# Sigmoid attention and two MoE layers: a conditional wait before the last scatter, sums of squares on VectorE, and two steps moved

## The chip, the core and the metric

The kernel runs on one core of one Trainium2 chip, as one program. Its time is the device time of one execution in microseconds (us), and less is better. The profile is of one execution; its times count from the first instruction. TensorE does the matmuls, VectorE and ScalarE the elementwise work, GpSimd some of it and the indirect DMA, and SP (SyncE) issues most DMAs.

## The reference

Four batches of 448 tokens pass through sigmoid attention (12 heads of 64), then through a first layer of experts that only tokens with a positive skip score enter, then through a second one for all tokens. Each token goes to one of eight experts and is scaled by that expert's gate. The second layer routes by normalized rows, which is where the sums of squares come from.

```
x = attention(q, k, v)                       # 1792 x 768
# layer 1: tokens with x @ w_skip > 0
e = argmax(xc @ w_gate);  y = gate_w * (relu(xc @ w1[e]) @ w2[e]);  out = x + y
# layer 2: all tokens
xn = x / (norm(x) + 1e-6);  en = emb / (norm(emb) + 1e-6)
e = argmax(xn @ en.T / tau);  out = gate_w * (relu(x @ v1[e]) @ v2[e])
```

With the reference's inputs nearly all tokens of a batch choose the same expert. In layer 1 no token of batches 0 and 1 is computed, all 448 of batch 2 go to expert 4, and of batch 3 407 go to expert 3 and 41 to expert 7. In layer 2 the four batches go to experts 5, 3, 6 and 2, but for 5 tokens of batch 2 that go to expert 1.

## The kernel before

**Dense blocks.** A batch's most frequent expert is computed for the whole batch, in a "dense block". The 1024 hidden columns come in eight groups f of 128. `h(f)` makes a group of the hidden layer (18 matmuls of 448 columns: six chunks, each in three products of high and low parts), ScalarE writes its high part `hh` (L820) and VectorE its low part `hl` (L821) out of a PSUM bank, and `y(f)` adds that group's share to six output banks `YS` (again 18 matmuls). The order in the code is the order on every engine; nothing is rescheduled:

```
h(f);  sub(2f);  y(f - 1);  sub(2f + 1)
```

So "step k" of a block is `sub(k)`: an even step stands between `h(f)` and `y(f - 1)`, an odd one between `y(f - 1)` and `h(f + 1)`. In the steps other work is issued: first the block's own weights (`units1`, `units2`: loads on SP, and L790 and L791, which split them into high and low parts on ScalarE and VectorE), then the lists that `merge` puts together, in the order given. Two PSUM banks (`BANKS`) serve `h` and all small matmuls of the steps. `bank()` hands them out in turn, so a second small matmul in one step gets the bank of the `h` just before it.

**Sums of squares.** For each batch `raw` copies the rows of x (ScalarE, L1098), `squares` squares six tiles of 128x448 (ScalarE, L1104), and `squares_sum` adds them into the tile `G` (GpSimd, five adds, L1108). The routing step `s1` (L250) reads `G` on TensorE. `route2_steps` returns the list of all that: three pieces `halves` (L702, L703), then `raw`, `squares`, `squares_sum`, `s1`, `s2`, `s3` (L293, L294, L296), `scaled_logits`, `gates`. `ROUTED` says at which steps of the second layer's blocks j = 0 and j = 1 the part from `raw` on stands for batches 1, 2 and 3; batch 0's sum stands at the end of the first dense block.

**The gate product.** In the second layer's blocks j = 0, 1, 2, `gate_tokens` builds the gates in the token order that the output needs: `ready` at step 3 (VectorE, L362 to L366, then L1359, which writes `SEL`), and `turned` at step 8 (TensorE L1366, which reads `SEL`, and a copy, L1368). GpSimd scales the block's output by it at the end (L1379). For j = 0, step 3 also holds a pair of `halves` pieces ahead of `ready`.

**Items.** Tokens that did not choose the batch's main expert are computed apart, in "items" of up to 64 or 32 tokens. `item_list` makes their list in three parts; part two ends with two VectorE operations L460, which write `SEL`, and part three reads that in four small matmuls (L468) and writes the list `LI` (L472 to L484). In the first dense block the parts stand at steps 10, 12 and 15; a batch's list entry is loaded by the engines when they decide which code runs next (L1263, behind the decision L1278). SP makes the same loads before it issues the next weights (L494, L499).

**The end.** The last block (j = 3) has a layer-2 item beside it. `finish_last` stores the batch in two halves (L1414), and `put` scales the item's rows (`xg`, L1028) and scatters them with an indirect DMA from GpSimd (L1029). An explicit dependency makes the scatter wait for the first store, and the tracking of `out` makes it wait for the second. Behind it stands the end of the If (L1494) and one more If for further items (L1506), which is empty here.

Of the kernel before, what the change touches and what calls it, by code (L numbers as in the profile page):

```python
# [14 lines left out]
ALU = mybir.AluOpType  # L15
AX = mybir.AxisListType
ENG = mybir.EngineType
# [4 lines left out]
def sigmoid_attention_moe_moe_kernel(  # L22
# [15 lines left out]
    nc = tc.nc  # L38
    B, H, S, D = q.shape
    NE, DM, DF = w1.shape  # L40
    NT = B * S
# [3 lines left out]
    ND = DM // 128  # L45
# [12 lines left out]
    raw = ctx.enter_context(tc.tile_pool(name="raw", bufs=1))  # L58
# [30 lines left out]
    K = {}  # L89
# [425 lines left out]
    def merge(*steps):  # L515

        out = {}
        for t in steps:
            for k in sorted(t):
                f = t[k]  # L520
                out.setdefault(k, []).extend(f if isinstance(f, list) else [f])
        return out
# [169 lines left out]
    R1, R2 = Route(0), Route(1)  # L692
# [169 lines left out]
    def halves():  # L862

        hw = DM // 2
        n = TL[0]
        for t in range(2):
            r, o = slice(n * t, n * t + n), slice(t * hw, t * hw + hw)
            nc.scalar.activation(YW[:n, o], YS[0][r, :hw], AF.Copy, scale=GS[r, 0:1])
        for t in range(2):
            r, o = slice(n * t, n * t + n), slice(t * hw, t * hw + hw)  # L870
            nc.vector.scalar_tensor_tensor(
                YW[n:, o], YS[0][r, :hw], GS[r, 0:1], YW[:n, o].bitcast(F32), op0=ALU.mult, op1=ALU.subtract
            )

    def spread(b):

        for d in range(ND):
            ps = YS[d]
            nc.tensor.matmul(ps[:, :S], lhsT=YW[:, d * 128 : (d + 1) * 128], rhs=SELT, start=True, stop=True)
            xd = batch_cols(d, b)  # L880
            nc.vector.tensor_add(xd, xd, ps[:, :S])
# [7 lines left out]
    class Item:  # L889
# [127 lines left out]
                            start=s + g + i == 0, stop=ng * s + g + i == 4,  # L1017
                        )

        def put(self):  # L1020
            if self.m == 0:
                halves()
                spread(self.b)
                return
            w = DM // self.ng
            nc.vector.scalar_tensor_tensor(IDX, GS[:, 1:2], float(self.ng), K["pc"][:, 7:8], op0=ALU.mult, op1=ALU.add)
            yg = spare()[:, :w]
            nc.vector.tensor_scalar(yg, YS[0][:, :w], GS[:, 0:1], None, op0=ALU.mult)  # L1028
            sc = nc.gpsimd.indirect_dma_start(  # L1029
                out=out.rearrange("n (t d) -> (n t) d", t=self.ng),  # L1030
                out_offset=bass.IndirectOffsetOnAxis(ap=IDX[:, 0:1], axis=0),
                in_=yg, in_offset=None, bounds_check=self.ng * NT - 1, oob_is_err=False,
            )
            return sc

        def ready(self, k0):

# [58 lines left out]
    def raw(b):  # L1096
        for p in range(ND):
            nc.scalar.activation(XR[:, p], batch_cols(p, b), AF.Copy)  # L1098

    SQ = ROW[:, : ND * S].rearrange("p (c s) -> p c s", s=S)  # L1100
# [3 lines left out]
            nc.scalar.activation(SQ[:, p], XR[:, p], AF.Square)  # L1104

    def squares_sum():
        for p in range(1, ND):
            nc.gpsimd.tensor_tensor(K["G"], K["G"] if p > 1 else SQ[:, 0], SQ[:, p], op=ALU.add)  # L1108

    def batch_of(j):  # L1110
        return nc.values_load(K["pb"][0:1, 8 + j : 9 + j], engines=XENG, min_val=0, max_val=B - 1)
# [32 lines left out]
    def next_dense(j):  # L1144

        box = {}
        xs = XST[(j + 1) % 2]

        def start():
            box["b"], box["e"] = rest_regs(j)  # L1150
            load1(w1, box["e"], 0)
            load2(w2, box["e"], 0)
            gate_cols(R1, box["b"])

        def rows():
            gate_rows(bank("ps_G"))
            box["p"] = split_gated(xs, box["b"])
            for p in range(2):
                box["p"](p)

        def last():
            load_unit(w1, w2, box["e"], 1)
            for f in split_unit(0)[:3]:
                f()

        return {
            8: start, 10: rows, 11: lambda: [box["p"](p) for p in (2, 3)], 12: lambda: [box["p"](p) for p in (4, 5, 6)], 13: last,
            14: lambda: [f() for f in split_unit(0)[3:]],
        }
# [115 lines left out]
    def item_steps(R, at):  # L1285
        return at_subs(at, item_list(R))
# [21 lines left out]
    with tc.If(na > 0) as cmp:  # L1308
        b, e = FIRST["b"], FIRST["e"]
        early = {0: s1, 2: s2, 4: s3, 5: [pl[0], lambda: gates(R1, B - 1, B)()], 6: pl[1], 7: pl[2]}  # L1310
        dense(XST[0], beside(units1(e), early), 0, NF // 2)
        NB["n"] = nb_load()
        with tc.If(NB["n"] > 0) as cmp2:
            steps = merge(next_dense(0), item_steps(R1, (10, 12, 15)), {12: lambda: raw(batch_of(0)), 15: squares})
            dense(XST[0], beside(units1(e), steps), NF // 2)
            add_y(b)
            squares_sum()
            block1(1)
        with cmp2.Else():
            steps = merge(rest2(), item_steps(R1, (9, 11, 12)))  # L1320
            dense(XST[0], beside(units1(e), steps), NF // 2)
            add_y(b)
            leftovers_now(lambda: start2(True))
            rare()
# [27 lines left out]
    def gate_tokens(j, box):  # L1352

        a = SEL[:P, :128]

        def ready():
            g = dense_gate(R2, j)
            four = [P, 4, C, 8]
            nc.vector.tensor_tensor(  # L1359
                a.rearrange("p (g c r) -> p g c r", g=4, r=8), g.unsqueeze(1).unsqueeze(3).to_broadcast(four),  # L1360
                K["seg"][:P].unsqueeze(1).unsqueeze(1).to_broadcast(four), op=ALU.mult,
            )

        def turned():
            ps = bank("ps_gt")
            nc.tensor.matmul(ps[:, :NK], lhsT=a, rhs=K["off"][:P], start=True, stop=True)  # L1366
            t = box["gt"] = sm.tile([128, NK], F32, tag="gtt", name="gtt", bufs=1)
            nc.vector.tensor_copy(t, ps[:, :NK])  # L1368

        return {3: ready, 8: turned}  # L1370

    def finish(j, b, gt):

# [18 lines left out]
    def finish_last(j, b):  # L1392
# [54 lines left out]

    pend, STORES = None, []
    ROUTED = {
        0: [(1, (1, 2, 2, 5, 6, 8, 10, 11)), (2, (7, 7, 7, 11, 12, 14, 15, 15))],  # L1450
        1: [(3, (3, 7, 7, 9, 10, 12, 13, 15))],
    }
    assert B == 4
    for j in range(B):
        box = {"e": e}
        last = j == B - 1
        if last:
            todo = {}
        else:
            todo = at_subs((3, 5, 7), route2_steps(j + 1, XST[(j + 1) % 2])[:3])  # L1460
            for n, at in ROUTED.get(j, ()):
                todo = merge(todo, at_subs(at, route2_steps(n, None)[3:]))
            todo = merge(todo, gate_tokens(j, box))
        if j == 0:
            load_unit(v1, v2, e, 1)
            halves()
            for f in split_unit(0, FIRST_RAW)[3:]:
                f()
            todo = merge({-0.5: lambda: spread(item_b())}, todo)
        if j == B - 2:  # L1470
            todo = merge(todo, item_steps(R2, (9, 11, 13)))
        if pend:
            todo = merge({2: pend}, todo)

        def units2(k):
            u, r = k // 4, k % 4
            if r == 0 and u + 2 < NU:
                load_unit(v1, v2, box["e"], u + 2)
            if k == 10 and not last:
                box["n"] = expert_of(j + 1)  # L1480
                load_unit(v1, v2, box["n"], 0)
            if (u + 1 < NU or not last) and r % 2 == 0:
                for f in split_unit((u + 1) % NU)[:3] if r == 0 else split_unit((u + 1) % NU)[3:]:
                    f()
            if k == 12 and not last:
                load_unit(v1, v2, box["n"], 1)

        xs = XST[j % 2]
        if not last:
            dense(xs, beside(units2, todo))  # L1490
            pend = finish(j, b, box["gt"])
            b, e = nc.values_load(K["pb"][0:1, 9 + j : 10 + j], engines=[ENG.SP], min_val=0, max_val=B - 1), box["n"]
            continue
        with tc.If(count(R2) > 0) as cmp:  # L1494
            it = Item(1, 0)
            at, prep = it.ready(0)
            steps = schedule(merge(todo, at), prep, (5, 5, 7))
            dense(xs, beside(units2, steps), end=finish_last(j, b))
            it.finish([None] * 3)
            info = mybir.DependencyInfo(mybir.DependencyClass.Sync, mybir.DependencyReason.DATA)  # L1500
            tc.add_manual_dep(it.put().ins, STORES[0].ins.name, info, reason="the rows it lands on")
        with cmp.Else():
            STORES = []
            dense(xs, beside(units2, todo), end=finish_last(j, b))
# [36 lines left out]
```

## Time and profile before

| | us |
|---|---|
| median of three timed runs | 561.24 (561.08 to 562.42) |
| profiled execution | 561.57 |
| its span, first to last instruction | 559.7 |
| TensorE matmul busy | 541.7 (97%) |
| VectorE busy | 296.8 (53%) |
| ScalarE busy | 251.2 (45%) |
| GpSimd busy | 79.5 (14%) |

The 1.87 us between span and time lie around the profiled instructions. The page names the engines PE (TensorE matmul), PEld (weight load), DVE (VectorE), ACT (ScalarE), POOL (GpSimd) and SP; a "q" behind the name is the engine's sequencer. A busy TensorE is one whose matmuls overlap, so the waits in brackets, and the spacing of starts, tell more than the busy share. The first attention stage lasts until about 150 us, the first layer until about 290, the second until the end.

### The profile page before, as it was taken

What the parts mean: (1) busy time and instruction counts of PE and PEld (TensorE: products, weight loads), DVE (VectorE), ACT (ScalarE), POOL (GpSimd) and SP (SyncE); (2) the same over time, 40 slices, a digit from 0 to 9 for tenths busy, and PEclk for the clock granted to TensorE, in tenths of its full rate; (3) what the DMA queues carried; (4) which work ended last, traced back from release to release, by engine and by line L of the source; (5) the groups of instructions that cost most, each with busy time, mean ns of one, the idle gap of its engine ahead of it and who ended that gap; (6) DMA issues with size and microseconds to landing.
All of it is one profiled execution on the core that took longest, in us unless ns stands there. A gap on an engine that the chain in (4) does not pass through costs nothing. (4 is left out here: it accounts for less than half of the span.)

```text
span 559.7 us, 10157 instructions
## 1 busy us (share of the span) xinstructions
PE 541.7 (97%) x3663; PEld 424.9 (76%) x3663; DVE 296.8 (53%) x794; ACT 251.2 (45%) x407; POOL 79.5 (14%) x153
## 2 busy tenths in 40 slices
PE   8999999999999998999989989999999999999993
PEld 5564644545489887899759878999899998989882
DVE  3734435246858676673138757694486534543221
ACT  5766776766932473231118543175133422222120
POOL 5010000000000013363002240043003000305000
PEclk9999999999999999999999999999999999999998
DMA  9868566764360603334557006227423832464263
GB/s 181 144 123 138 104 117 110 141 107 145 138 202 2 219 10 131 113 102 155 185 170 269 19 5 237 99 50 219 169 73 92 217 112 78 117 147 168 99 227 105
DMA packets 169244, 73.35 MB, mean 131 GB/s; under 512 B 134450, under 2 KB 160838, under 8 KB 169168
## 3 DMA queue, kind: packets, MB, share of 16 engines
q1 hardware_dynamic: 147440, 65.71, 43.7%
q10 hardware_dynamic: 21360, 6.20, 4.6%
q0 software_dynamic: 368, 0.53, 0.5%
q8 instruction: 36, 0.59, 0.4%
q14 instruction: 40, 0.33, 0.2%
HBM read 66.90 MB, written 5.60 MB: 130 GB/s over the span
## 5 line engine op out<-in xcount | busy, mean ns | idle before, releaser
L820 ACT ACTIVATE hh<-bank 128x448 fp32r<-128x448 f32 x48 | 26.1, 543 | 198.6 <-PE bank L802 168.5
L800 PE MATMUL bank<-xs,h 128*128 128x448 f32 x288 | 106.9, 371 | 2.5 <-DVE xT L1197 1.0
L800 PE MATMUL y<-hh,h 128*128 128x448 f32 x288 | 107.2, 372 | 0.0
L802 PE MATMUL bank<-xs,l 128*128 128x448 f32 x288 | 105.5, 366 | 1.0 <-issue 0.9
L802 PE MATMUL y<-hh,l 128*128 128x448 f32 x288 | 105.5, 366 | 0.0
L801 PE MATMUL y<-hl,h 128*128 128x448 f32 x288 | 105.4, 366 | 0.0
L801 PE MATMUL bank<-xs,h 128*128 128x448 f32 x288 | 105.3, 366 | 0.0
L821 DVE SCALAR_TENSOR_TENSOR hl<-bank,hh 128x448 fp32r<-128x448 f32 x48 | 29.9, 622 | 133.4 <-ACT hh L820 133.3
L621 ACT ACTIVATE A<-psS,bias 128x896 f32<-128x896 f32 x84 | 83.3, 1006 | 34.8 <-PE psS L617 34.5
L791 DVE TENSOR_TENSOR l<-r,h 128x512 fp32r<-128x512 f32 (+1 forms) x115 | 91.5, 844 | 3.7 <-ACT h L790 1.9
L617 PE MATMUL psS<-qT,kT 64*64 64x448 f32 x672 | 87.3, 541 | 0.5 <-ACT A L621 0.3
L635 PE MATMUL psO<-A,v 64*64 64x448 f32 x672 | 86.3, 539 | 0.0
L790 ACT ACTIVATE h<-r 128x512 fp32r<-128x512 f32 (+1 forms) x115 | 74.4, 708 | 0.0
L800 PEld LDWEIGHTS bank<-xs,h 128*128 128x128 f32 x288 | 54.1, 188 | 12.7 <-issue 5.2
L635 PEld LDWEIGHTS psO<-A,v 64*64 64x64 f32 x672 | 34.8, 133 | 32.2 <-issue 19.9
L800 PEld LDWEIGHTS y<-hh,h 128*128 128x128 f32 x288 | 54.1, 188 | 5.3 <-issue 0.6
L802 PEld LDWEIGHTS bank<-xs,l 128*128 128x128 f32 x288 | 54.1, 188 | 5.0 <-DVE l L791 0.4
L801 PEld LDWEIGHTS y<-hl,h 128*128 128x128 f32 x288 | 54.1, 188 | 4.7 <-issue 0.2
L802 PEld LDWEIGHTS y<-hh,l 128*128 128x128 f32 x288 | 54.1, 188 | 4.7
L801 PEld LDWEIGHTS bank<-xs,h 128*128 128x128 f32 x288 | 54.1, 188 | 4.3
L617 PEld LDWEIGHTS psS<-qT,kT 64*64 64x64 f32 x672 | 32.4, 132 | 30.6 <-issue 16.2
L1108 POOL TENSOR_TENSOR G<-row 128x448 f32<-128x448 f32 x4 | 5.1, 1264 | 250.3 <-ACT row L1104 233.6
(267 smaller groups left out, 449.8 us busy)
## 6 DMA issues: line engine op xcount, KB each, us to landing
r<-in_moe_w_dram SPq DMA_DIRECT2D x62, 768.0 KB, 4.7
k<-in_k_dram SPq DMA_DIRECT2D x44, 112.0 KB, 2.8
q<-in_q_dram SPq DMA_DIRECT2D x44, 112.0 KB, 3.1
v<-in_v_dram ACTq DMA_DIRECT2D x44, 112.0 KB, 2.8
out_dram<-row SPq DMA_DIRECT2D x12, 336.0 KB, 3.8
stg<-in_moe_w_dram SPq DMA_DIRECT2D x1, 768.0 KB, 6.9
row<-in_moe_w_dram SPq DMA_DIRECT2D x1, 768.0 KB, 7.8
out_dram<-row SPq DMA_DIRECT2D x1, 672.0 KB, 3.9
```

Source lines behind the costliest of these rows:

```text
L617: nc.tensor.matmul(ps[KT * i : KT * i + KT, j, :S], lhsT=kT[r, i, h * KT : (h + 1) * KT], rhs=qT[r, i], start=True, stop=True,)
L621: nc.scalar.activation(at, ps[:, :, :S], AF.Sigmoid, bias=bias, scale=1.0 / math.sqrt(D))
L635: nc.tensor.matmul(ST[w, "o"][i][D * j : D * j + D, :S], lhsT=t[r, j, h, :], rhs=at[r, j, :], start=h == 0, stop=h == NH - 1,)
L790: nc.scalar.activation(dst_h, src, AF.Copy)
L791: nc.vector.tensor_sub(dst_l, src, dst_h.bitcast(F32))
L800: nc.tensor.matmul(ps, lhsT=ah, rhs=bh, start=first, stop=False)
L801: nc.tensor.matmul(ps, lhsT=ah, rhs=bl, start=False, stop=False)
L802: nc.tensor.matmul(ps, lhsT=al, rhs=bh, start=False, stop=last)
L820: nc.scalar.activation(a, ps[:, :S], AF.Relu)
L821: nc.vector.scalar_tensor_tensor(l, ps[:, :S], 0.0, a.bitcast(F32), op0=ALU.max, op1=ALU.subtract)
L1108: nc.gpsimd.tensor_tensor(K["G"], K["G"] if p > 1 else SQ[:, 0], SQ[:, p], op=ALU.add)
```

## The change

Four edits. The item's scatter is taken out of `put` and issued in one of two branches on GpSimd: if the item belongs to the last batch, with the dependency on the stores as before, otherwise without any on them. `squares_sum` runs on VectorE, in three operations: one over half of the tiles at once (128x1344), and two of 128x448. The list's third part in the first dense block moves from step 15 to step 13. In the second layer's block j = 0 the gate product's `turned` moves from step 8 to step 4, and the sum for batch 2 from step 7 to step 9.

```diff
-        def put(self):
+        def put(self, scatter=True):
...
-            sc = nc.gpsimd.indirect_dma_start(
+            self.yg = yg
+            return self.scatter() if scatter else None
+
+        def scatter(self):
+            return nc.gpsimd.indirect_dma_start(
...
     def squares_sum():
-        for p in range(1, ND):
-            nc.gpsimd.tensor_tensor(K["G"], K["G"] if p > 1 else SQ[:, 0], SQ[:, p], op=ALU.add)
+        n = ND // 2
+        nc.vector.tensor_add(SQ[:, :n], SQ[:, :n], SQ[:, n:])
+        for p in range(1, n):
+            nc.vector.tensor_add(K["G"], K["G"] if p > 1 else SQ[:, 0], SQ[:, p])
...
-            steps = merge(next_dense(0), item_steps(R1, (10, 12, 15)), {12: lambda: raw(batch_of(0)), 15: squares})
+            steps = merge(next_dense(0), item_steps(R1, (10, 12, 13)), {12: lambda: raw(batch_of(0)), 15: squares})
...
-        return {3: ready, 8: turned}
+        return {3: ready, 8 if j else 4: turned}
...
-        0: [(1, (1, 2, 2, 5, 6, 8, 10, 11)), (2, (7, 7, 7, 11, 12, 14, 15, 15))],
+        0: [(1, (1, 2, 2, 5, 6, 8, 10, 11)), (2, (7, 7, 9, 11, 12, 14, 15, 15))],
...
             it = Item(1, 0)
+            own = nc.values_load(R2.LI[0:1, 0:1], engines=[ENG.Pool], min_val=0, max_val=B - 1)
...
             it.finish([None] * 3)
+            it.put(False)
             info = mybir.DependencyInfo(mybir.DependencyClass.Sync, mybir.DependencyReason.DATA)
-            tc.add_manual_dep(it.put().ins, STORES[0].ins.name, info, reason="the rows it lands on")
+            with tc.If(own > B - 2) as cmp2:
+                tc.add_manual_dep(it.scatter().ins, STORES[0].ins.name, info, reason="the rows it lands on")
+            with cmp2.Else():
+                sc = it.scatter()
+                for st in STORES:
+                    tc.declare_no_dep(sc.ins, st.ins, reason="rows of another batch")
```

## Rows read from the trace of the kernel before

**Rows 1.** The page, busy us (share of the span) and instructions of TensorE and others.

```profile
PE 541.7 (97%) x3663; PEld 424.9 (76%) x3663; DVE 296.8 (53%) x794; ACT 251.2 (45%) x407; POOL 79.5 (14%) x153
```

**Rows 2.** Timeline of TensorE, block j = 0: start, us, line, tiles, idle before.

```profile
307.82 0.36 PE L800 MATMUL y<-hh,h 128*128 128x448 f32 x1
...
324.77 0.39 PE L294 MATMUL bank<-OH,one 112*128 112x32 f32 x2
326.99 0.39 PE L1366 MATMUL bank<-off,sel 112*128 112x14 f32 x2 [1.83 <-DVE hl L821]
327.24 0.45 PE L800 MATMUL y<-hh,h 128*128 128x448 f32 x1
...
331.55 0.47 PE L800 MATMUL bank<-xs,h 128*128 128x448 f32 x1 [0.43 <-DVE tt L296]
```

**Rows 3.** Timeline of TensorE, the same place in block j = 1.

```profile
406.38 0.39 PE L294 MATMUL bank<-OH,one 112*128 112x32 f32 x2
406.60 0.45 PE L800 MATMUL y<-hh,h 128*128 128x448 f32 x1
```

**Rows 4.** Timeline of TensorE, first dense block and the seam to `block1`.

```profile
201.22 0.36 PE L800 MATMUL bank<-xs,h 128*128 128x448 f32 x1
...
213.87 0.44 PE L800 MATMUL bank<-xs,h 128*128 128x448 f32 x1 [0.96 <-DVE xT L1197]
...
216.03 0.36 PE L802 MATMUL bank<-xs,l 128*128 128x448 f32 x1 [0.91 <-issue]
```

**Rows 5.** Timeline of VectorE, the list of the first layer's items.

```profile
201.85 0.53 DVE L460 TENSOR_SCALAR sel<-io,ilf 128x64 f32<-128x64 f32 x2
...
212.14 1.03 DVE L484 CAST LI<-ilm 1x4 int32<-1x4 f32 x1
```

**Rows 6.** The chain that ended last, its last piece: start, us, what.

```profile
555.62 0.89 POOL out_dram L1029
```

**Rows 7.** Timeline of VectorE and of GpSimd at the end.

```profile
550.72 0.42 DVE L1028 TENSOR_SCALAR xg<-y,small 128x192 f32<-128x192 f32 x1 [1.78 <-PE y L1014]
...
555.40 1.10 POOL L1029 DMA_INDIRECT out_dram<-xg,small  x1 [39.13 <-SPq L1506]
```

**Rows 8.** The scatter's line L1029, from issue to landing.

```profile
DMA to landing us min/median/max: 2.9/2.9/2.9
```

**Rows 9.** Lines L1494 and L1506, TensorE's sequencer: ns min/median/max, first to last start.

```profile
L1494 PEldq COMPARE_BRANCH  x2: 73/2558/5043, 478.4 to 549.4; - x2
...
L1506 PEldq COMPARE_BRANCH  x1: 3119/3119/3119, 555.0 to 555.0; - x1
```

**Rows 10.** Timeline of VectorE, blocks j = 0 and j = 1.

```profile
306.49 2.49 DVE L703 TENSOR_TENSOR xs<-xT,xs 128x448 fp32r<-128x448 f32 x2 [1.74 <-ACT xs L702]
...
311.30 0.29 DVE L1359 TENSOR_TENSOR sel<-dg,seg 112x128 f32<-112x128 f32 x1
...
313.85 0.62 DVE L703 TENSOR_TENSOR xs<-xT,xs 128x448 fp32r<-128x448 f32 x1
...
372.50 1.14 DVE L703 TENSOR_TENSOR xs<-xT,xs 128x448 fp32r<-128x448 f32 x2
...
374.22 0.29 DVE L1359 TENSOR_TENSOR sel<-dg,seg 112x128 f32<-112x128 f32 x1
...
384.33 0.95 DVE L791 TENSOR_TENSOR l<-r,h 128x768 fp32r<-128x768 f32 x1
```

**Rows 11.** Timeline of ScalarE, the squares of batch 1 in block j = 0.

```profile
303.09 2.90 ACT L1104 ACTIVATE row<-stg 128x448 f32<-128x448 f32 x6
```

**Rows 12.** Line L1278, TensorE's sequencer.

```profile
L1278 PEldq COMPARE_BRANCH  x1: 3796/3796/3796, 209.0 to 209.0; - x1
```

**Rows 13.** Timeline of SP, first weight load of `block1`.

```profile
214.27 0.38 SPq L494 DMA_DIRECT2D r<-in_moe_w_dram  x1
```

**Rows 14.** Two stretches: us, busy by engine (instructions), granted clock, DMA share, GB/s.

```profile
209.00:212.80 3.80, 3.80 (x20) 3.30 (x18) 3.48 (x10) 1.00 (x3) 3.56 (x4) 1.00 0.02 6
549.40:554.50 5.10, 1.18 (x32) 0.65 (x20) 0.42 (x1) 0.00 (x0) 0.00 (x0) 1.00 0.47 141
```

More of the change, by code (lines that the diff above doesn't have):

```diff
@@ L1028, in put @@
             nc.vector.tensor_scalar(yg, YS[0][:, :w], GS[:, 0:1], None, op0=ALU.mult)
-            sc = nc.gpsimd.indirect_dma_start(
+            self.yg = yg
+            return self.scatter() if scatter else None
+        def scatter(self):
+            return nc.gpsimd.indirect_dma_start(
                 out=out.rearrange("n (t d) -> (n t) d", t=self.ng),
                 out_offset=bass.IndirectOffsetOnAxis(ap=IDX[:, 0:1], axis=0),
-                in_=yg, in_offset=None, bounds_check=self.ng * NT - 1, oob_is_err=False,
+                in_=self.yg, in_offset=None, bounds_check=self.ng * NT - 1, oob_is_err=False,
             )
-            return sc
         def ready(self, k0):
```

## The prediction

> **What bounds the kernel now.** I read the page first: TensorE is busy for 541.7 of 559.7 us [rows 1], so the time moves only where TensorE waits, or behind its last matmul. I therefore went through TensorE's timeline by the "idle before" in brackets, and then, for each place that the diff touches, through VectorE, ScalarE and GpSimd beside it. Three places count.
>
> First, the second layer's first dense block (j = 0). There the gate product's matmul L1366 at step 8 waits 1.83 us for VectorE's `hl`, since the routing matmuls L293 and L294 just took the other bank; it starts at 326.99 though L294 ran at 324.77. A little later the next `h` waits 0.43 us for L296, which is late on VectorE [rows 2]. In the next block (j = 1) the step after L294 starts 0.22 us behind it [rows 3]: that is the spacing without a wait.
>
> Second, the seam from the first dense block to `block1`: TensorE stops for 0.96 and, five matmuls on, for 0.91 us [rows 4]. The first is put down to VectorE's L1197; the register load of L1263 stands there too, and the list that it reads is only written by L484, which ends at 213.17 [rows 5].
>
> Third, the end. The chain that ended last is the scatter alone [rows 6]: GpSimd idles for 39.13 us and issues it at 555.40, while its data (`xg`) stands at 551.14 [rows 7], and it lands 2.9 us later [rows 8], at 558.3. But TensorE, whose matmuls are over, is not done either: its jump at the end of the If (L1494) takes 5.04 us, to 554.5, and the jump over the last If (L1506) 3.12 us from 555.0, to 558.15 [rows 9].
>
> **The change part by part.**
>
> *The scatter's wait.* In the reference's data the one item of the second layer holds five rows of batch 2, and the last block is batch 3, so the branch without the wait is taken. The scatter can then go from 551.2 on and land by about 554.1 to 555. What is late next is TensorE's second jump, 558.15 against 558.3: I take -0.1. The new branch stands on GpSimd, behind the gathers and some 35 us ahead of the data, so its load and jump are covered by that same 39 us. The bounds are 0 and, if the two jumps also became shorter, 558.3 - 555 = -3.3. The Trainium skill (NRT & Kernel Launch, "Instruction fetch mechanics") states that a taken branch with its target outside the fetched window waits for a DMA of the target page; the two jumps of 5.04 and 3.12 us agree, and the rule speaks against any gain here.
>
> *The sums of squares.* Four times, five GpSimd adds become three VectorE adds. A 128x768 operation of this kind takes 0.95 us and a 128x448 one 0.62 [rows 10], so 1.03 ns per column: the first add (1344 columns) costs 1.56, the other two 0.62 each, 2.8 us together. VectorE has room, and a late `hl` is covered: y(f) reads it only after a block of y and a block of h, each about 3.9 us (y from 327.24, the next h due at 331.1 [rows 2]). So three of the sums (batch 0 at the seam, batch 2 at step 9, batch 3 at step 7) I cost at nothing; without that cover each costs up to 2.8. The one for batch 1 at step 2 stands in front of something, next. In exchange the operations beside GpSimd's adds get quicker: the pair of L703 took 2.49 us there and 1.14 elsewhere [rows 10]. The Trainium skill (SBUF — State Buffer, "Who interferes with whom") says that a VectorE instruction with two SBUF inputs contends with a GpSimd instruction that reads SBUF, and the pair agrees; by that rule alone one would forecast a gain, which is the second rival below.
>
> *The gate product from step 8 to step 4 for j = 0.* What goes: y(3) starts at 324.99 instead of 327.24, -2.25, and since one bank less is taken there, the next h no longer follows L296: -0.43 [rows 2, 3]. What comes: step 4 stands right behind h(2), which ends as y(1) starts, at 307.82 [rows 2]. The product reads what L1359 writes in step 3, and in the kernel before L1359 ended at 311.59 [rows 10]; that held nothing up, as TensorE wanted it only at step 8. Now VectorE's order is: sum of squares (step 2), a pair of L703, three small operations and L1359. ScalarE's last square ends at 305.99 [rows 11]. Add 2.8 for the sum, 308.8; the pair and the products behind it took 2.01 where GpSimd was idle (372.50 to 374.51 [rows 10]), 310.8. TensorE then takes L1366, and y(1) 0.25 later (326.99 to 327.24 [rows 2]): 311.05 instead of 307.82, **+3.2**. Bounds: if the adds were free, 308.0 for the product, so +0.4; if pair and products ran as slowly as beside GpSimd's adds (306.49 to 311.59, 5.1 us [rows 10]), 313.9 and +6.3. I stay near the quick end, since what ran beside them is gone.
>
> *The list's third part from step 15 to step 13 (first layer).* Its four matmuls L468 now stand between y(5) and h(7), which starts at 201.22 [rows 4]. They read what the two L460 write, and these end at 202.38 on VectorE, which has no slack ahead of them [rows 5]. So h(7) is held about **+1.2**; the matmuls themselves cost the same in either place. Bounds: 0 (the list were ready) and +1.5. What the earlier list gives: L484 moves up by some 5 us, so the register load at the seam finds it. Of the 0.96 us this could return 0.3 (213.17 against the jump's end: L1278 starts at 209.0 and takes 3.80, to 212.8 [rows 12]). I count it at 0, because the stop five matmuls later waits for no data ("issue") and would take up what comes earlier.
>
> *What the earlier list sets off.* SP waits for the same list, and its next weight loads start 1.1 us behind it, at 214.27 [rows 13]. They move to about 209, in front of TensorE's jump, which shifts to about 210.2. Before, the DMA share during that jump was 0.02, and the jump took 3.80; the jump at L1494, with the last store in flight, had a share of 0.47 and took 5.04 [rows 9, 12, 14]. The difference is 1.24. TensorE runs out of matmuls just as this jump ends, so each tenth more is idle time. I take **+1.0**, near the row with traffic; bounds 0 and, with two loads in flight instead of one store, 2.5.
>
> *The step of batch 2's sum (7 to 9)* only keeps VectorE from waiting for the squares in front of `hl`; nothing.
>
> **The sum**: -0.1 + 3.2 - 2.25 - 0.43 + 1.2 + 1.0 = +2.6 us. It is made against the profiled execution (span 559.7, 561.57 with what lies around it); that execution is 0.33 above the median of 561.24, so I put the change on the median: **563.8 us**.
>
> **The rivals.**
>
> *The jump is not delayed* (the loads start later than I think, or leave room): +1.6, 562.8 us. For it: no row shows a jump beside weight loads. Against it: the 5.04 of L1494 beside a store.
>
> *Faster: the two moved pieces are ready when TensorE gets there.* Then only what goes is left: -2.25 - 0.43 - 0.1 + 0.25 for L1366 in its new place = -2.5, 558.7 us. The point that decides is L1359 before 307.8, three microseconds earlier than my chain. For it: free of GpSimd's adds VectorE's pair alone gains 1.3 us. Against it: the last square ends only at 305.99, and behind that the sum, the pair and the products are 4.8 us in one queue. If the end fell by 3.3 as well or instead, this case grows.
>
> *One of the two waits is missing*: without the product's 2.6 - 3.2 + 0.25 = -0.35 (560.9), without the list's +1.4 (562.6).
>
> *The jump waits for both loads*: 2.5 instead of 1.0, 565.3 us and above.
>
> *The change does not do what it says*: were the branch with the wait taken, only the -0.1 would go.
>
> **How the numbers follow.** A measurement of this kernel tells about 0.3% (1.7 us) from no change. My forecast gets 0.46 (all of it slower, 562.95 to 564.7); no delay of the jump 0.22 (0.08 slower, 0.14 within); one wait missing 0.13 (0.12 within, 0.01 slower); neither wait or a shorter end 0.12 (faster); both loads 0.07 (slower). That makes slower 0.62, within 0.26, faster 0.12. The range reaches down to one wait missing and up to the jump behind both loads, 560.8 to 565.6, and leaves out the faster case and a little above.
>
> **What would show it.** L1366 of j = 0 behind h(2) with some 3 us idle and VectorE's L1359 as its releaser; no wait at step 8 and none before h(5). L468 ahead of h(7) with 1.2 us idle put down to L460. SP's load at the seam near 209, ahead of TensorE's jump of L1278, and that jump longer than 4 us. The scatter issued near 552, the span's last microsecond unchanged behind TensorE's L1506. No G adds on GpSimd, and L703 at 0.6 each. I am wrong if L1366 finds its product, if the jump stays at 3.8, or if the two jumps at the end shrink.

## The result, and the profile after

The changed kernel takes 568.74 us (median of 5 runs, 566.19 to 569.53) beside 561.84 (561.08 to 563.09) for the kernel before: a ratio of 1.0111 [1.0082, 1.0140], slower. (Ratios here are of means, with 95% intervals.) The forecast was 563.8 with a range of 560.8 to 565.6, so the side was right and the size was not: 6.9 us more instead of 2.6. The profiled execution took 569.53, its span is 567.7, 8.0 more than before. It is the slowest of the five, so what is read from it adds up to somewhat more than the 6.9 of the medians.

The page of the changed kernel, busy us and share of the span:

```profile
PE 547.2 (96%) x3663; PEld 428.9 (76%) x3663; DVE 298.5 (53%) x806; ACT 251.2 (44%) x407; POOL 54.5 (10%) x133
```

The same 3663 matmuls are busy 5.5 us longer than before [rows 1]. A wait can't do that. Work or clock must have changed, and the matmuls are the same.

TensorE's timeline after, first layer (L1202 was L1197):

```profile
201.92 0.49 PE L468 MATMUL bank<-sel,pc 128*1 128x64 f32 x4 [0.83 <-DVE sel L460]
...
216.02 0.46 PE L800 MATMUL bank<-xs,h 128*128 128x448 f32 x1 [2.44 <-DVE row L1111]
...
216.86 0.57 PE L800 MATMUL bank<-xs,h 128*128 128x448 f32 x1
...
218.72 0.74 PE L800 MATMUL bank<-xs,h 128*128 128x448 f32 x1 [0.54 <-issue]
```

and in the second layer's block j = 0 (L1371 was L1366):

```profile
315.92 0.61 PE L1371 MATMUL bank<-off,sel 112*128 112x14 f32 x2 [2.90 <-DVE sel L1364]
316.36 0.72 PE L800 MATMUL y<-hh,h 128*128 128x448 f32 x1
...
336.09 0.39 PE L294 MATMUL bank<-OH,one 112*128 112x32 f32 x2
336.31 0.45 PE L800 MATMUL y<-hh,h 128*128 128x448 f32 x1
...
340.10 0.36 PE L800 MATMUL bank<-xs,h 128*128 128x448 f32 x1
```

The waits stand where they were forecast: a new one of 0.83 us at L468 for L460, 2.44 instead of 0.96 at the seam, and a new one of 2.90 at the gate product for the operation that writes its operand (L1364, L1359 before). The stop that followed the seam's first one shrinks from 0.91 to 0.54 us. The two old waits, at step 8 and at the next h [rows 2], are gone. But look at the second number of each line: behind 2.44 and behind 2.90 a matmul of 448 columns takes 0.57 and 0.72 instead of 0.36 and 0.45. Windows of the changed kernel say why; the columns are us, busy by engine, granted clock, DMA share, GB/s:

```profile
209.80:215.40 5.60, 3.78 (x19) 3.17 (x17) 4.82 (x7) 1.38 (x3) 0.00 (x0) 1.00 0.81 278
216.55:223.38 6.83, 6.29 (x18) 5.07 (x17) 0.48 (x1) 0.00 (x0) 0.00 (x0) 0.50 0.02 5
315.54:322.36 6.82, 6.44 (x18) 5.79 (x19) 3.78 (x8) 0.54 (x2) 0.00 (x0) 0.50 0.00 0
324.60:331.40 6.80, 6.80 (x36) 6.23 (x35) 2.10 (x3) 3.15 (x6) 0.00 (x0) 1.00 0.00 0
```

From 0.5 us behind the one stop, and from 0.4 us ahead of the end of the other, the granted clock stands at 0.50, which is 1.2 of 2.4 GHz, for 6.8 us each: 18 matmuls instead of the 36 of the last line. In the profiled execution of the kernel before it stands at 1.00 from 5.5 to 555 us without a break.

SP's load and TensorE's jump at the seam (L1283 was L1278), in the changed kernel:

```profile
208.56 0.39 SPq L494 DMA_DIRECT2D r<-in_moe_w_dram  x1
```

```profile
L1283 PEldq COMPARE_BRANCH  x1: 5616/5616/5616, 209.8 to 209.8; - x1
```

The load is issued at 208.56 instead of 214.27 [rows 13], the DMA share during the jump is 0.81 instead of 0.02 [rows 14], and the jump takes 5.62 instead of 3.80 us [rows 12].

VectorE in the second layer, from the sum to the product's operand:

```profile
311.05 1.56 DVE L1111 TENSOR_TENSOR row<-row 128x1344 f32<-128x1344 f32 x1 [1.27 <-ACT row L1107]
312.64 0.62 DVE L1113 TENSOR_TENSOR G<-row 128x448 f32<-128x448 f32 x1
313.30 0.62 DVE L1113 TENSOR_TENSOR G<-G,row 128x448 f32<-128x448 f32 x1
313.85 1.15 DVE L703 TENSOR_TENSOR xs<-xT,xs 128x448 fp32r<-128x448 f32 x2
...
315.57 0.29 DVE L1364 TENSOR_TENSOR sel<-dg,seg 112x128 f32<-112x128 f32 x1
```

This is the forecast queue, with the forecast durations: 2.8 us of sums, and a pair that takes 1.15 instead of 2.49 [rows 10]. The Trainium skill (SBUF — State Buffer, "Who interferes with whom") puts such a pair's slowness down to GpSimd's reads; the trace agrees, the gain is there, and the product still comes 2.9 us late.

The end, GpSimd's scatter and TensorE's two jumps:

```profile
560.47 1.10 POOL L1033 DMA_INDIRECT out_dram<-xg,small  x1 [35.55 <-DVE xg L1028]
```

```profile
L1508 PEldq COMPARE_BRANCH  x1: 5123/5123/5123, 557.9 to 557.9; - x1
...
L1518 PEldq COMPARE_BRANCH  x1: 2744/2744/2744, 563.5 to 563.5; - x1
```

The scatter now waits for `xg` alone and lands 2.7 us later, at 563.2; TensorE's second jump ends at 566.2. The time moved out of the scatter, and TensorE's code is last.

The account in the profile: how far the starts of TensorE's blocks stand behind those of the kernel before, step by step.

| step | forecast, us | measured, us |
|---|---|---|
| list part at step 13 (L468), with the 0.14 by which the first layer starts early | +1.2 | +0.8 |
| jump at the seam (+1.4), and the second stop (0.54 instead of 0.91 us) | +1.0 | +1.1 |
| **clock at half behind the seam** | none | **+2.8** |
| until the second layer | 0 | +0.3 |
| gate product at step 4 | +3.2 | +3.5 |
| **clock at half behind the product** | none | **+2.8** |
| step 8, the next h | -2.7 | -2.8 |
| until TensorE's last block, and the end | -0.1 | -0.5 |
| sum | +2.6 | +8.0 |

Without the two lines in bold the measured sum is 2.4.

### The profile page after: what moved, and what is told of

It reads as the page before. It is cut to its first block, busy times and chain, and to the rows that moved or that the text cites. A ratio compares the mean times of both kernels' runs of the same rounds, so it can differ in the third digit from the quotient of the medians.

```text
span 567.7 us, 10128 instructions
## 1 busy us (share of the span) xinstructions
PE 547.2 (96%) x3663; PEld 428.9 (76%) x3663; DVE 298.5 (53%) x806; ACT 251.2 (44%) x407; POOL 54.5 (10%) x133
## 4 chain that ended last, share of the span: by engine, by line
PE 88%; DVE 4%; ACT 3%; DMA 2%; issue 2%; DVEq 0%; POOL 0%; SPq 0%; POOLq 0%; ACTq 0%
PE y L800 10%; PE psS L617 10%; PE bank L800 10%; PE y L801 10%; PE y L802 10%; PE psO L635 10%; PE bank L802 10%; PE bank L801 10%; PE y L1014 1%; PE bank L989 1%; DMA r<-in_moe_w_dram 1%; PE bank L250 1%; ACT A L621 1%; DMA k<-in_k_dram 1%; PE ps_r L250 1%
## 5 line engine op out<-in xcount | busy, mean ns | idle before, releaser
L800 PE MATMUL bank<-xs,h 128*128 128x448 f32 x288 | 108.2, 376 | 4.4 <-DVE row L1111 2.4
L800 PE MATMUL y<-hh,h 128*128 128x448 f32 x288 | 108.4, 376 | 0.0
L802 PE MATMUL bank<-xs,l 128*128 128x448 f32 x288 | 106.7, 370 | 0.1
L801 PE MATMUL bank<-xs,h 128*128 128x448 f32 x288 | 106.3, 369 | 0.0
L791 DVE TENSOR_TENSOR l<-r,h 128x512 fp32r<-128x512 f32 (+1 forms) x115 | 87.4, 809 | 3.5 <-ACT h L790 1.9
L800 PEld LDWEIGHTS bank<-xs,h 128*128 128x128 f32 x288 | 54.9, 190 | 13.9 <-issue 5.6
L801 PEld LDWEIGHTS bank<-xs,h 128*128 128x128 f32 x288 | 54.8, 190 | 4.5
L965 POOL COPY row<-xT 128x6 f32 x64 | 18.4, 307 | 216.8 <-PE bank L800 204.8
```

Of the source, the lines that this page charges most:

```text
L791: nc.vector.tensor_sub(dst_l, src, dst_h.bitcast(F32))
L800: nc.tensor.matmul(ps, lhsT=ah, rhs=bh, start=first, stop=False)
L801: nc.tensor.matmul(ps, lhsT=ah, rhs=bl, start=False, stop=False)
L802: nc.tensor.matmul(ps, lhsT=al, rhs=bh, start=False, stop=last)
L965: nc.gpsimd.tensor_copy(self.xb[:, :, t : t + 1], xT[:, :, ds(o, 1)])
```

## The experiments

Each was timed beside the kernel before, whose medians were 561.70 to 562.20.

**One part back at a time.** `e1_turned8` is the changed kernel with the product back at step 8, `e2_list15` with the list part back at step 15, `e3_both_back` with both back, `e4_turned7` as the third, but with the product at step 7.

```diff
-            steps = merge(next_dense(0), item_steps(R1, (10, 12, 13)), {12: ...
+            steps = merge(next_dense(0), item_steps(R1, (10, 12, 15)), {12: ...      # e2, e3, e4
-        return {3: ready, 8 if j else 4: turned}
+        return {3: ready, 8: turned}                    # e1, e3
+        return {3: ready, 8 if j else 7: turned}        # e4
```

> The changed kernel with the gate product's turned back at step 8 for j = 0; the list part stays at step 13. Theory W (each long stop of TensorE costs its own length and then 6.8 us at half the granted clock): the stop of 2.9 us at L1371 and the fall of the clock behind it go (-3.5 and -2.8), the 1.8 us wait of step 8 and some of the 0.4 before h(5) come back (+2.3 to 2.7). The seam keeps its stop and its fall. About 3.5 to 4 us below the changed kernel, 565 us, one fall of the clock. Rival S (the sums on VectorE are what costs, and the clock falls of itself): no clear gain, about 568, falls in any number.

Measured 566.52, ratio 1.0068 [1.0044, 1.0093]. The product's wait is gone, but the 1.83 us at step 8 are back, and behind them, too, the clock is at half, for 3.4 us. The time lies between the two that were expected.

> The changed kernel with the list's third part back at step 15. Theory W: the wait at L468 (0.9 net), the longer jump at the seam (1.4) and the fall of the clock behind it (2.9) go, and the jump of L1283 is back near 3.8 us: about 5 us below the changed kernel, 563.5, one fall, behind the product's stop. Rival S: about 568. Rival J (only the traffic beside the jump costs, the falls are no part of it): 1.4 to 2.3 less, 566.5.

Measured 567.82, 1.0090 [1.0061, 1.0118]. The jump is back at 3.70 us, and yet nothing is won at the seam: five matmuls on, where the kernel before stops for 0.91 us [rows 4], TensorE stops for 3.74, and the clock falls for 6.8 us. (At the product it stops for 2.85 us, and here the clock falls for 3.4.) The first theory missed, and the time is that of its rival, that the sums cost.

> The changed kernel with both moved pieces back (list part at 15, turned at 8): what is left are the scatter's branch, the sums on VectorE and the step 7 to 9. Theory W: no stop over 2 us, no fall of the clock; the end gains 0.1 to 0.4, the wait of 0.43 before h(5) may shrink: 561 to 561.8, the same as before. Rival S: 564 or more.

Measured 566.03, 1.0064 [1.0043, 1.0084]. What is left of the change, the scatter's branch and the sums on VectorE, should by the forecast have cost nothing; it costs 4 us, as the rival had it. In the profile 3.5 us of that come at the seam (a second stop of 3.39 us, and the clock for 3.4 us). Another 1.0 net comes at step 8, where the clock now falls behind the old wait:

```profile
331.40:334.81 3.41, 3.41 (x11) 3.02 (x11) 3.17 (x17) 0.46 (x1) 0.00 (x0) 0.50 0.02 5
```

> As e3_both_back, but with turned at step 7 for j = 0, where no other small matmul takes a bank and the product has long been written. Theory W: the 2.25 of step 8 and the 0.43 before h(5) go and nothing comes but the matmul's own 0.25: 2.2 to 2.8 below the kernel before, 559.1 to 559.6, no fall. Rival S: not below the kernel before.

Measured 561.47, 0.9986 [0.9971, 1.0001]. That misses the 559.1 to 559.6 expected. In the profile the seam costs 4.7 us here; step 7 waits for nothing, and the 1.83 us and the clock behind them are gone, which pays for it: the median is that of the kernel before. The second stop in `e4_turned7`:

```profile
217.88 0.53 PE L802 MATMUL bank<-xs,l 128*128 128x448 f32 x1 [3.73 <-issue]
```

**Each part alone, on the kernel before.**

```diff
+        n = ND // 2                                      # e7: squares_sum as in the change, 7 to 9
+        nc.vector.tensor_add(SQ[:, :n], SQ[:, :n], SQ[:, n:])
...
+            steps = merge(next_dense(0), item_steps(R1, (10, 12, 13)), ...     # e5
+        return {3: ready, 8 if j else 4: turned}         # e6
+            with tc.If(own > B - 2) as cmp2:             # e8: the scatter in two branches, as in the change
```

> The kernel before with the sums of squares on VectorE (and the one step moved from 7 to 9), nothing else. If taking the adds off GpSimd makes the list part shorter and so the loads about 2 us earlier, this alone has the long second stop (3.4 to 3.7 us, 0.9 before) and the fall of the clock, and the time is 565 to 567, as e3_both_back. If the sums cost nothing, as the prediction had it, the time is 561 to 562.5 and the stop of e3_both_back comes from the branch at the end of the kernel (another size of code).

Measured 566.44, 1.0078 [1.0059, 1.0098]. SP, VectorE and TensorE in `e7_only_sums`:

```profile
212.34 0.38 SPq L494 DMA_DIRECT2D r<-in_moe_w_dram  x1
```

```profile
211.08 0.16 DVE L484 CAST LI<-ilm 1x4 int32<-1x4 f32 x1
```

```profile
218.55 0.50 PE L802 MATMUL bank<-xs,l 128*128 128x448 f32 x1 [3.47 <-issue]
```

The list's last operation took 1.03 us and ended at 213.17 beside GpSimd's adds [rows 5]; now it takes 0.16 and ends at 211.24. SP's load follows it, 1.93 us earlier than before, and the stop grows from 0.91 to 3.47. So an edit that takes work away from GpSimd moves a DMA on SP's queue, and TensorE stops longer. In the profile 3.6 us come at the seam and 0.9 from a fall of the clock behind the wait of step 8, as in `e3_both_back`.

> The kernel before with the list part at step 13 instead of 15, nothing else: GpSimd keeps its adds, but they start at 208.2 us, when the list part is nearly through, so the loads should be issued near 209 as in the changed kernel. By the theory of the loads: a jump of 5.0 to 5.6 us (3.8 before), a stop near 2.4 us, the clock at half behind it, 564.5 to 567. By the prediction's own terms for this part (+1.2 and +1.0): 563 to 564.5, with no fall of the clock. If the loads have nothing to do with the jump: 561.5 to 563.

Measured 567.35, 1.0090 [1.0063, 1.0118]. The jump and the stop behind it, and the window behind both, in `e5_only_list13`:

```profile
L1278 PEldq COMPARE_BRANCH  x1: 5579/5579/5579, 209.7 to 209.7; - x1
```

```profile
215.92 0.46 PE L800 MATMUL bank<-xs,h 128*128 128x448 f32 x1 [2.39 <-issue]
```

```profile
216.75:223.57 6.82, 5.75 (x17) 4.61 (x16) 0.00 (x0) 0.00 (x0) 0.00 (x0) 0.50 0.02 5
```

With the load at 208.49 this one moved line makes the whole stop of the changed kernel, on the sums' old engine. There the profile put the stop down to the sum L1111; here it is "issue", the same stop without that sum. The name in the bracket was not the cause.

> The kernel before with the gate product moved from step 8 to step 4 in the first round of the second layer, nothing else. The prediction's terms alone: wait of 2.9 to 3.4 us at step 4, step 8's 2.25 and the 0.43 gone, so +0.3 to +0.8 in the profile: 562 to 563. With the fall of the granted clock behind a stop of that length, 2 to 3 us more: 564 to 566, and the records show the clock at half for some microseconds right behind the wait.

Measured 564.86, 1.0061 [1.0044, 1.0079]. The wait and the clock in `e6_only_turned4`:

```profile
311.75 0.40 PE L1366 MATMUL bank<-off,sel 112*128 112x14 f32 x2 [3.59 <-DVE sel L1359]
```

```profile
313.40:316.81 3.41, 3.41 (x11) 3.02 (x10) 1.78 (x5) 0.00 (x0) 0.00 (x0) 0.50 0.00 0
```

In the profile the wait puts the block back by 4.0 us, and step 8 and the next h give 2.8 back: 1.2 net, where under 1 was expected. The 3.41 us at the half clock add 1.6.

> The kernel before with the branch around the scatter, nothing else. The prediction gives it -0.1 us: 561.3 to 562.2, nothing to be seen beside the time before. If the other code at the end of the program moves the fetches of the seam or the jump at the start of the last block: over 563. If the scatter was on the chain of the end after all: 559.5 to 561.

Measured 561.22, 0.9984 [0.9968, 1.0000]: the same, or up to 1.8 us less. Its seam is that of the kernel before (0.97 and 0.97 us).

The single parts add up to more than the whole (5.15 + 4.66 + 3.08 - 0.98 = 11.9, against 6.9), since list and sums both lead to the same stop, and each alone also keeps the wait of step 8, with a fall of the clock behind it in its profile.

**Only the loads moved.** A tiny write into the tile that the first load fills holds SP back, and nothing else. In `e10_late_load` (on `e4_turned7`) and `e11_after_late` (on the changed kernel) it stands behind the first sum:

```diff
         nc.vector.tensor_add(SQ[:, :n], SQ[:, :n], SQ[:, n:])
+        if held:
+            nc.vector.memset(RAW_T[0][0][:, 0, 0:1], 0.0)
```

> e4_turned7 with one tiny VectorE write into the tile that the first weight load of the next block fills, put behind the first tree sum after the seam: the load can then be issued only at about 215.1 us (211.3 in e4_turned7, 214.3 before). If the early load is what delays TensorE's code at the seam, the second stop there is about 0.9 us and not 3.7, the granted clock stays up behind it, and the time falls by 3 to 5 us from e4_turned7's 561.5, to 556.5 to 558.5. If the stop comes from the code itself (its size or place), or from the emptied VectorE, the stop stays at 3.4 to 3.7 us and the time at 561 to 562. If the load, now later than before, is late for its splits, a wait on VectorE or ScalarE shows in the next block and the time is over 562.

Measured 560.62, 0.9983 [0.9971, 0.9994]. TensorE's timeline in `e10_late_load`:

```profile
215.76 0.37 PE L802 MATMUL bank<-xs,l 128*128 128x448 f32 x1 [1.41 <-issue]
...
223.97 0.96 PE L250 MATMUL bank<-stg,wr 128*32 128x224 f32 x16 [1.73 <-DVE hl L821]
```

The stop falls from 3.73 to 1.41, the clock stays at 1.00, and the block's second group of matmuls starts 4.3 us earlier than in `e4_turned7`. But the time falls by 0.9 only. In the profiles 2.5 of the 4.3 are left, and the profiled run of `e4_turned7` (563.16) lies 1.7 above its median, so the medians show 0.9. The held load, issued at 215.60, now meets the jump of another engine: VectorE branches at 216.54 and goes on at 222.67, 6.1 us later (214.37 and 218.40 before), so `hl` is late and TensorE waits 1.73 us for it:

```profile
223.29 0.62 DVE L821 SCALAR_TENSOR_TENSOR hl<-bank,hh 128x448 fp32r<-128x448 f32 x1 [6.54 <-ACT hh L820]
```

The expected 556.5 to 558.5 was missed.

> The changed kernel with the same tiny write: only the loads move, list part at step 13 and gate product at step 4 stay. If the early loads make the jump at the seam long, it falls from 5.6 us to 3.6 to 3.9, the stop there from 2.44 to under 1.2 us, the clock does not fall behind it, and the time goes from 568.7 to 563.5 to 565.5; what is left over the time before is then the product's wait (2.9 us) and the clock behind it. If the jump is long for another reason, the time stays at 568 to 569.

Measured 566.29, 1.0085 [1.0068, 1.0103]. The jump is back at 3.46 us, the second stop is 1.34, but the clock falls for 3.4 us behind it all the same; the time came down by 2.5 us, less than expected, and the product's wait (2.91, with 6.8 us at half speed) is untouched.

`e12_hold_early` has the write ahead of the sums; `e13_sums_inside` has the sums behind the branch besides, in step 0 of the next block.

```diff
             add_y(b)
+            nc.vector.memset(RAW_T[0][0][:, 0, 0:1], 0.0)    # e12, e13
             squares_sum()                                    # not in e13
             block1(1)
...
+            return at_subs((0, 1, 4, 6, 2, 3, 5, 6, 8), [squares_sum] + f[:3] + f[6:])   # e13
```

> As e10_late_load, but the tiny write stands ahead of the tree sums, right behind the sixth add of y: SP can issue the first load at about 213.6 us. In e10_late_load the held load met VectorE's own jump instead (its branch at 216.54, its next instruction at 222.67, 6.1 us; 4.0 before), and TensorE waited 1.73 us for it. If any engine's code that is asked for while the weights flow comes late, the load at 213.6 leaves TensorE's second stop between 0.9 us (asked before the flow) and 3.7 us, and VectorE's jump at 3.6 to 4.5 us, with no wait of TensorE behind it: 558 to 560. If TensorE's stop is back at 3.7 us: 561.5, as e4_turned7.

Measured 560.17, 0.9966 [0.9956, 0.9976]: faster. TensorE's timeline in `e12_hold_early`, with SP's load at 213.99:

```profile
215.80 0.36 PE L802 MATMUL bank<-xs,l 128*128 128x448 f32 x1 [1.28 <-issue]
...
222.97 0.96 PE L250 MATMUL bank<-stg,wr 128*32 128x224 f32 x16 [0.69 <-DVE hl L821]
```

VectorE's jump takes 5.2 us here, more than the 3.6 to 4.5 expected, and costs 0.69; the time is just above the expected range.

> As e12_hold_early, with the sums of squares moved behind the branch, to step 0 of the next block: VectorE reaches its branch at about 214 us, as before, so that its code is asked for ahead of the weights too. By the theory both stops at the seam are as before (about 0.9 us each), the clock stays, VectorE goes on at about 218, and the gate product at step 7 gives its 2.4 us: 558 to 559.5. If the 2.8 us of sums behind the jump come before the subtraction of h that TensorE needs, a wait of 1 to 2.5 us shows at the first y of the block: 559.5 to 561.5.

Measured 561.65, 1.0001 [0.9989, 1.0012]. VectorE's jump is back at 3.1 us (212.85 to 215.98), as the theory has it, but the routing matmuls now wait 1.43 us for `G`, and L953 1.38: the sums' 2.8 us have no cover there. This is the second of the two outcomes expected, a little above its range.

**What is left of the change.** `e14_no_sums` is the kernel before with the scatter's branch and the product at step 7 for j = 0.

```diff
-        return {3: ready, 8: turned}
+        return {3: ready, 8 if j else 7: turned}
```

> The kernel before with the branch around the scatter and the gate product at step 7 in the first round of the second layer; the sums stay on GpSimd and the list part at step 15, so the loads at the seam should be issued at 214.3 us as before. By the theory both stops of the seam stay under 1.1 us, the product waits for nothing at step 7 (its operand is written near 311 us, step 7 is near 322) and the waits of 1.83 and about 0.4 us behind step 8 go: 2.3 to 2.8 us less than e8_only_scatter, 558.4 to 559.5. If the gain of step 7 came with the sums on VectorE, the 1.83 us stay and the time is 561 to 562.

Measured 558.23 (557.63 to 558.58), 0.9931 [0.9912, 0.9950]: faster than both kernels. TensorE's timeline in `e14_no_sums`:

```profile
215.60 0.36 PE L802 MATMUL bank<-xs,l 128*128 128x448 f32 x1 [0.58 <-issue]
...
320.88 0.29 PE L1369 MATMUL bank<-off,sel 112*128 112x14 f32 x2
...
324.92 0.39 PE L294 MATMUL bank<-OH,one 112*128 112x32 f32 x2
325.14 0.45 PE L800 MATMUL y<-hh,h 128*128 128x448 f32 x1
```

No bracket stands at the product, nor behind L294, where the kernel before waits 1.83 us. The seam is as before, with SP's load at 214.17.

## Why the prediction was right on the side and wrong on the size

**The mechanisms came as forecast.** The waits at L468 and at the product, the earlier load and the longer jump, the two waits that go, and the scatter's end are all in the account above, each within 0.5 us of its term. The term for the jump, +1.0 against +1.1, owes part of that to luck: the jump itself grew by 1.8 us, which lies between the 1.24 of the row with traffic and the 2.5 of the rival with both loads, and the second stop gave 0.3 back, which the prediction didn't count. (The column price gives 1.54 us, not 1.56, for the first add; the 2.8 of the sums stand.) The rivals without a delay of the jump, or without one of the waits, are refuted by their rows, and so is the faster one: VectorE's queue was quicker, as its rule had it, but not by the three microseconds that decide.

**The step that failed** is the sum. It takes every wait at its own length and every matmul at the length of [rows 2], and has no term for TensorE's granted clock behind a wait. Behind the stops of 2.44 and 2.90 us the clock stood at half for 6.8 us each, and that cost 2.8 and 2.8, together 5.6, where forecast and account differ by 5.4 us. The "-2.25" for step 8 was read in the same way, and `e1_turned8` shows that such a wait can bring a fall with it. The kernel before may be no exception: of the 84 executions timed beside the experiments 32 have a mean granted clock of 0.993 and a mean time of 562.5, and 26 have 0.996 and 561.1. The six of `e14_no_sums`, without the wait at step 8, all have 0.995 to 0.997; this fits a fall behind that wait in part of the runs, but no profile of the kernel before caught one. What decides whether a stop is followed by a fall, and for how long, stays open. Long stops differ: at the product 3.4 us follow a stop of 2.85 in `e2_list15`, and 6.8 one of 2.90 in the changed kernel. So do short ones: behind the 1.83 us at step 8 the profiles of the kernel before and of `e8_only_scatter` show none, those of `e1_turned8`, `e3_both_back`, `e5_only_list13` and `e7_only_sums` one of 3.4 us, and behind the stop at the seam there is one in `e11_after_late` (1.34 us) and none in `e10_late_load` (1.41).

**A second step was wrong, and the sum did not show it.** The prediction costs three of the sums at nothing, since a late `hl` is covered. The cover was real, but the sum at the seam has another price: with GpSimd's adds gone, the list's small operations are quick, and SP's load follows the list. `e7_only_sums` puts the sums alone at 4.7 us (566.44 against 561.78), 3.6 of them at the seam in its profile. In the changed kernel the list part at step 13 had moved the load in front of the jump already, so the account has no line for it. The prediction saw the chain from list to load to jump for the one edit and did not follow it for the other.

**That the loads are the cause at the seam** is shown by holding them back alone (`e10_late_load`, `e11_after_late`, and `e12_hold_early` against `e4_turned7`), which takes the long stop or the long jump away. Two unlike edits that bring them forward, the list's in `e5_only_list13` and the sums' in `e7_only_sums`, each bring one:

| kernel | SP's load, us | weights flow, us | instruction queue's records, us | jump, us | second stop, us | clock at half, us |
|---|---|---|---|---|---|---|
| before | 214.27 | 215.3 to 221.1 | 210.5, 213.6 | 3.80 | 0.91 | 0 |
| changed | 208.56 | 209.6 to 216.4 | 213.0, 216.2 | 5.62 | 0.54 | 6.8 |
| `e5_only_list13` | 208.49 | 209.6 to 216.3 | 212.9, 216.1 | 5.58 | 1.07 | 6.8 |
| `e7_only_sums` | 212.34 | 213.4 to 219.9 | 210.5, 216.3 | 3.60 | 3.47 | 3.4 |
| `e4_turned7` | 211.28 | 212.3 to 219.0 | 209.5, 215.7 | 3.74 | 3.73 | 6.8 |
| `e12_hold_early` | 213.99 | 215.1 to 220.7 | 209.8, 213.2 | 3.64 | 1.28 | 0 |

The second stop stands five or six matmuls behind the jump. The weights are the two loads of L494 and L499. The records are those of DMA queue q8 (16 KB each), and the table gives their starts; they are read as code on its way. Where the weights flow first, the record that falls into the flow comes later, late in the flow, and the stop that waits for it is longer by about as much: 2.7 us later and 3.47 against 0.91 us at the second stop, 1.7 us later and 5.6 against 3.8 at the jump. Which engine a record belongs to the trace doesn't name, but the times fit TensorE closely: in all 15 kernels the jump ends 1.36 to 1.38 us after the first record has ended, and the second stop ends 1.2 to 1.5 us after the second one has. The Trainium skill (Runtime: NRT & Kernel Launch, "Instruction fetch mechanics") says that a taken branch to a page outside the fetched window waits for a DMA; the table agrees, and what it adds is that this DMA comes late beside other transfers.

## What to carry to other kernels

A wait of two or three microseconds on TensorE can cost twice its length (2.90 us at the product put the block back by 3.5 and cost 2.8 more), as the clock behind it may fall to half: price a new stop with that, look at the granted clock of the window behind it, and value the removal of an old stop likewise. An earlier input is no gain where it releases a large load: follow the load to what shares the DMA engines with it, the code of the engines' next branch above all, on TensorE and on VectorE. And if a bundle of edits loses, time each part alone: here two of them lost at one place, and the one that was to move to step 4 gained at step 7.

## What was not expected of the hardware

- Code behind a branch comes late beside flowing weights: TensorE's jump took 5.1 to 5.6 us with the list part at step 13 and the loads free, 3.4 to 3.8 otherwise; its second stop 3.4 to 3.7 us beside the loads, 0.6 to 1.4 ahead of them, and 0.5 to 1.2 behind a late jump; VectorE's jump 6.1, 5.9 and 5.2 in `e10_late_load`, `e11_after_late` and `e12_hold_early`, 2.9 to 4.8 elsewhere.
- The granted clock stood at 0.50 for 3.4 or 6.8 us behind, or late in, stops of 1.34 to 3.7 us, in the middle of an execution in which TensorE is busy for 96%.
- VectorE operations on a few elements can slow down beside GpSimd's adds as well: L484, with four elements, took 1.03 us there and 0.16 without them.
